# x loaded in fp32 by SyncE and cast on chip, with the constants first on GpSimd, in an attention and Fourier-mixing FFN kernel

## The chip, the cores and the metric

The kernel runs on one core of a Trainium2 chip. The metric is the device time of one execution in microseconds (us); runs are repeated and their median is taken. The engines are TensorE (PE; PEld is its weight load), VectorE (DVE), ScalarE (ACT), GpSimd (POOL) and SyncE (SP). Each has one queue of instructions that it takes in order, and a DMA stands in the queue of the engine that issues it.

## The reference

Eight batches, each with H = 8 heads of S = 512 rows of D = 64, and 32 state rows per head. First cross attention in both directions, then a mixing block over the 544 rows of 512 columns that result: the real part of a two-dimensional Fourier transform is added, the sum is normalised, and an FFN of width 2048 follows.

```python
scores = scale * np.matmul(x, state.transpose(0, 1, 3, 2))      # a  = softmax(scores)
xread = np.matmul(a, state)
scores2 = scale * np.matmul(state, x.transpose(0, 1, 3, 2))     # a2 = softmax(scores2)
sread = np.matmul(a2, x)
y = np.concatenate([xread, sread], axis=2)                      # heads side by side: (8, 544, 512)
mixed = np.real(np.fft.fft(np.fft.fft(y, axis=1), axis=2))
u = y + mixed
un = (u - mean(u)) / np.sqrt(var(u) + 1e-06)
out = u + np.maximum(un @ w_ch1, 0.0) @ w_ch2
```

## The kernel before

A batch goes through `front(b)` and then `ffn(b)`. The loop calls, for each b, `load_x(b + 2)`, `front(b + 1)` and `ffn(b)`; after batches 3 and 7 a small `front_low` and `ffn` handle the low-frequency rows of four batches together. The program is written with a scheduler that orders the instructions of each engine when the kernel is built, by the dependencies and its own idea of the times; the order on an engine is then fixed. So an instruction may stand in its queue ahead of one that the text has earlier, as the load of x for batch b + 2 does.

x is held in two buffers `xin` in bf16, [128, 4, 514]: four groups of 128 rows, with a column of ones at either end for the sums of the softmax. `load_x` (L64 to L74) fills one by five DMAs on GpSimd's queue that convert fp32 to bf16 on the way. Row 0 of x goes to partition 0 of group 2, so that group is loaded as a one-row and a 127-row piece; the others are whole 128-row pieces. The weights w1 and w2 are converted in the same way (L84, L87: four DMAs and two).

`front(b)` transposes the state and x on TensorE (`sTp` L219, `xTp` L228, with the identity matrix `ident`), copies the results to `sT` and `xT`, and computes the scores both ways (`eTp`, `esp`), the exponentials on ScalarE (`ET`, `E`), and the reads (`srp` L260, the last use of `xin`, and `xfp`, `xrp`, `xlp` L271). VectorE normalises these to XF, XR and XL and folds them into `Sm`, XE and XO (L303 to L308). GpSimd copies two columns of `Sm` and one of XL into `XN` (L306, L309). The first Fourier transform is the matmuls `gep` (L317) and `gop` (L323, and L327 with XN) against cosine and sine tables CT, ST, CL, SL; ScalarE copies them to G. The second is `yp` (L338) against T2. VectorE adds this into U (three buffers, L332), takes statistics (GpSimd finishes `rstd`, L202 and L203) and subtracts the mean; TensorE transposes (`tp`, L352) and ScalarE copies to `unT` (three buffers).

`ffn` (L387) computes 64 matmuls `ph` (L393) into `hT` (two buffers), with the ReLU on ScalarE and VectorE, and 64 matmuls `po` (L402) in four tiles. VectorE makes `ot` from `po`, `rstd` and U (L405, three buffers), and SyncE stores it, half of the tiles by way of the scratch tensor `r_dram` (L408 to L415).

At the start, GpSimd's queue has in the text `load_x(0)`, the w1 loads, `load_x(1)`, the w2 loads, the identity (L90), small constants (L110 to L115), the clears of CL and SL, the index tables by `iota` (L126 to L132), and the clears of all XF, XR, XL, XE, XO and XN buffers (L177). VectorE turns the indices into angles (`turn`, L140 to L151) in scratch of a pool `gen` of its own, and ScalarE takes the sines (L156 to L165).

Of the kernel before, what the change touches and what calls it, by code (L numbers as in the profile page):

```python
# [28 lines left out]
def kernel(  # L29
# [80 lines left out]
    epst = singles.tile([128, 1], F32, name="epst")  # L110
    nc.gpsimd.memset(epst, eps)
    mhalf = singles.tile([128, 1], F32, name="mhalf")
    nc.gpsimd.memset(mhalf, -0.5)
    halfpi = singles.tile([128, 1], F32, name="halfpi")
    nc.gpsimd.memset(halfpi, PI / 2)  # L115
# [3 lines left out]
    with tc.tile_pool(name="gen", bufs=1) as gen:  # L119
        pi_ = gen.tile([128, 5], I32, name="pi_")  # L120
        pf = gen.tile([128, 5], F32, name="pf")
        li = gen.tile([128, dm], I32, name="li")
        l1 = gen.tile([128, NM], F32, name="l1")
        l2 = gen.tile([128, dm], F32, name="l2")
        lt = gen.tile([128, NM], I32, name="lt")
        nc.gpsimd.iota(pi_[:, 0:3], pattern=[[128, 3]], base=1, channel_multiplier=1)  # L126
        nc.gpsimd.iota(pi_[:, 3:5], pattern=[[128, 2]], base=0, channel_multiplier=1)
        for hh in range(4):
            nc.gpsimd.iota(pi_[32 * hh:32 * hh + 32, 2:3], pattern=[[0, 1]], base=256, channel_multiplier=1)  # L129
        nc.gpsimd.iota(lt[:, 0:256], pattern=[[1, 256]], base=1, channel_multiplier=0)  # L130
        nc.gpsimd.iota(lt[:, 256:NM], pattern=[[1, NL]], base=256, channel_multiplier=0)
        nc.gpsimd.iota(li, pattern=[[1, dm]], base=0, channel_multiplier=0)  # L132
        nc.vector.tensor_copy(pf, pi_)  # L133
        for hh in range(4):
            nc.vector.memset(pf[32 * hh:32 * hh + 1, 2:3], 0.0)
        nc.vector.tensor_copy(l1, lt)
        nc.vector.memset(l1[:, 256:257], 0.0)
        nc.vector.tensor_copy(l2, li)

        def turn(W, N, lf, cols, name):  # L140
            n = len(cols)
            f = gen.tile([128, n, W], F32, name=f"f{name}")
            q = gen.tile([128, n, W], F32, name=f"q{name}")
            for i, c in enumerate(cols):
                nc.vector.tensor_scalar(f[:, i, :], in0=lf, scalar1=pf[:, c:c + 1], scalar2=None, op0=ALU.mult)
            nc.vector.tensor_scalar(q, in0=f, scalar1=1.0 / N, scalar2=float(1 << 23), op0=ALU.mult, op1=ALU.add)
            nc.vector.tensor_scalar(q, in0=q, scalar1=float(1 << 23), scalar2=-float(N), op0=ALU.subtract, op1=ALU.mult)
            nc.vector.tensor_add(f, f, q)
            nc.vector.tensor_scalar(q, in0=f, scalar1=-1.0, scalar2=None, op0=ALU.mult)
            nc.vector.tensor_max(q, q, f)  # L150
            return f, q  # L151

        shrink = 1.0 - 1e-6
        f, q = turn(NM, Stot, l1, [0, 1, 2], "1")
        w = 2.0 * PI / Stot * shrink
        nc.scalar.activation(CT, q[:, 0:2, :], AF.Sin, bias=halfpi, scale=-w)  # L156
        nc.scalar.activation(ST, f[:, 0:2, :], AF.Sin, bias=0.0, scale=w)
        for hh in range(4):
            pq = slice(32 * hh, 32 * hh + 32)
            nc.scalar.activation(CL[pq, hh, :], q[pq, 2, :], AF.Sin, bias=halfpi[pq], scale=-w)  # L160
            nc.scalar.activation(SL[pq, hh, :], f[pq, 2, :], AF.Sin, bias=0.0, scale=w)
        f, q = turn(dm, dm, l2, [3, 4], "2")
        w = 2.0 * PI / dm * shrink
        nc.scalar.activation(T2[:, 0:2, :], q, AF.Sin, bias=halfpi, scale=-w)
        nc.scalar.activation(T2[:, 2:4, :], f, AF.Sin, bias=0.0, scale=-w)  # L165
        alt = T2[0:1, 2, :].rearrange("p (n two) -> p two n", two=2)
        nc.vector.memset(alt[:, 0, :], 1.0)
        nc.vector.memset(alt[:, 1, :], -1.0)


    def fixed(name, shape, dt, n=2, fill=0.0):
        ts = []
        for i in range(n):
            t = singles.tile(shape, dt, name=f"{name}{i}")
            letters = "abcd"[:len(shape) - 1]
            flat = t.rearrange(f"p {' '.join(letters)} -> p ({' '.join(letters)})") if len(shape) > 2 else t
            nc.gpsimd.memset(flat, fill)  # L177
            ts.append(t)
        return ts
# [26 lines left out]
    def front(b):  # L206
# [125 lines left out]
        U = wk.tile([128, 2, 2, 514], F32, name="U", tag="U", bufs=3)  # L332
        unT = wk.tile([128, DC, 512], BF16, name="unT", tag="unT", bufs=3)
# [122 lines left out]
```

## Time and profile before

| | us |
|---|---|
| median of 3 runs | 660.19 (660.08 to 660.78) |
| profiled execution, its own time | 664.54 |
| its span, first to last instruction | 661.0 |
| TensorE busy in it | 359.5 (54%), mean granted clock 0.829 |
| VectorE, ScalarE, GpSimd busy | 205.1, 130.2, 133.2 |

The busy time of TensorE is modelled for pipelined matmuls and is no measure of how near it is to its peak. GpSimd's 133.2 us hold the time in which it issues DMAs. A wait is put down to the engine that ended it; "issue" stands for time in which an engine waited for nothing that the profile shows. A line such as L327 is a line of the kernel; where one row covers several instructions, xN gives their number.

### The profile page before, as it was taken

The numbers are of one execution on the slowest core, as the hardware profiler recorded it, in microseconds if no ns is written. First come the engines' busy times: TensorE is split into PE (matmuls) and PEld (weight loads), VectorE is DVE, ScalarE is ACT, GpSimd is POOL, SyncE is SP. The second block draws the span as 40 slices with busy tenths as digits, with TensorE's granted clock in tenths as the row PEclk, the third lists the DMA queues.
The fourth block names the chain that finished last, engine by engine and source line by source line (L and its number), as shares of the span: only waits on it lengthen the run. The fifth ranks groups of instructions, "written<-read, shape, count | busy, mean of one in ns | idle before, by whom it ended". The sixth has DMA issues, their size and how long they took to land.

```text
span 661.0 us, 5124 instructions
## 1 busy us (share of the span) xinstructions
PE 359.5 (54%) x1973; PEld 181.7 (27%) x2008; DVE 205.1 (31%) x470; ACT 130.2 (20%) x217; POOL 133.2 (20%) x170
## 2 busy tenths in 40 slices
PE   0000104138349907960990767237599949989970
PEld 0000102015124403530440326014244424434440
DVE  1000095034224604440560333413451463331220
ACT  4000033014111402410350114001123411313010
POOL 4134463222411311240241111411010001000000
PEclk9999997557859956995895788558589979999995
DMA  6592662422331362243126212440020003001210
GB/s 79 10 120 6 51 90 16 10 11 16 7 13 63 50 10 10 17 61 30 8 17 11 40 48 14 41 15 16 1 78 19 1 1 112 0 34 62 90 67 35
DMA packets 170680, 22.83 MB, mean 35 GB/s; under 512 B 158112, under 2 KB 166304, under 8 KB 170656
## 3 DMA queue, kind: packets, MB, share of 16 engines
q0 software_dynamic: 159584, 8.88, 23.9%
q1 hardware_dynamic: 11072, 13.63, 5.7%
q8 instruction: 15, 0.25, 0.2%
q14 instruction: 9, 0.07, 0.0%
HBM read 21.50 MB, written 13.11 MB: 52 GB/s over the span
## 4 chain that ended last, share of the span: by engine, by line
PE 40%; issue 35%; POOL 13%; DVE 7%; ACT 2%; POOLq 0%; DVEq 0%; ACTq 0%
PE po L402 17%; PE ph L393 13%; POOL xin L74 10%; PE yp L338 3%; PE tp L352 1%; PE gop L323 1%; PE gop L327 1%; DVE XR L295 1%; DVE st L198 1%; PE eTp L237 1%; PE srp L260 1%; PE xTp L228 1%; ACT E L254 1%; DVE U L340 1%; DVE XF L278 1%
## 5 line engine op out<-in xcount | busy, mean ns | idle before, releaser
L74 POOL DMA_DIRECT2D xin<-in_x_dram x40 | 79.4, 1993 | 247.2 <-issue 181.1
L393 PE MATMUL ph<-unT,w 128*128 128x512 bf16 x496 | 125.9, 392 | 2.2 <-ACT hT L398 0.7
L402 PE MATMUL po<-w,hT 128*128 128x512 bf16 x532 | 121.8, 382 | 3.9 <-DVE ot L405 3.0
L398 ACT ACTIVATE hT<-ph 128x512 bf16<-128x512 f32 (+1 forms) x120 | 63.2, 535 | 111.7 <-PE ph L393 90.4
L393 PEld LDWEIGHTS <-w 128*128 128x128 bf16 x640 | 60.5, 102 | 61.9 <-issue 15.2
L402 PEld LDWEIGHTS <-hT 128*128 128x128 bf16 x544 | 53.5, 98 | 67.7 <-issue 6.1
L327 PE MATMUL gop<-CT,XN 128*128 128x288 bf16 x16 | 5.3, 438 | 118.4 <-POOL XN L306 118.4
L396 DVE TENSOR_SCALAR hT<-ph 128x512 bf16<-128x512 f32 (+1 forms) x40 | 24.2, 604 | 132.6 <-PE ph L393 125.9
L219 PE MATMUL sTp<-ident,stb 128*128 128x128 bf16 x32 | 3.7, 250 | 79.9 <-POOL ident masks.py:199 79.4
L340 DVE TENSOR_TENSOR U<-yp,XF 128x512 f32<-128x512 f32 x16 | 11.1, 691 | 115.8 <-PE yp L338 115.7
L327 PEld LDWEIGHTS <-XN 128*128 128x128 bf16 x24 | 2.5, 127 | 121.8 <-POOL XN L306 120.7
L405 DVE SCALAR_TENSOR_TENSOR ot<-po,rstd,U 128x512 f32<-128x512 f32 x32 | 23.2, 746 | 38.9 <-PE po L402 38.8
L202 POOL TENSOR_TENSOR rstd<-mv,epst 128x1 f32<-128x1 f32 x34 | 6.6, 195 | 135.4 <-DVE mv L200 134.9
L354 ACT COPY unT<-tp 128x512 bf16<-128x512 bf16 x32 | 17.4, 588 | 77.7 <-PE tp L352 77.6
L328 ACT CAST G<-gop 128x576 bf16<-128x576 f32 x8 | 5.1, 638 | 127.8 <-PE gop L323 127.8
L219 PEld LDWEIGHTS <-stb 128*128 128x128 bf16 x32 | 2.8, 112 | 81.0 <-issue 73.5
L133 DVE CAST pf<-pi__121 128x5 f32<-128x5 int32 x1 | 0.2, 172 | 77.4 <-POOL pi__121 L129 77.4
L338 PE MATMUL yp<-T,G 128*128 128x512 bf16 x57 | 21.9, 485 | 2.4 <-ACT unT L354 1.1
L237 PE MATMUL eTp<-xT,sT 128*128 128x288 bf16 (+1 forms) x64 | 11.5, 310 | 20.7 <-DVE xT L229 20.4
L203 POOL TENSOR_TENSOR rstd<-rstd,mhalf 128x1 f32<-128x1 f32 x34 | 21.3, 626 | 2.7
L198 DVE BATCH_NORM_STATS2 st<-U 128x6 f32<-128x512 f32 x32 | 20.4, 681 | 0.0
L352 PE MATMUL tp<-ident,ub 128*128 128x128 bf16 x128 | 12.8, 243 | 14.0 <-DVE ub L349 13.8
(108 smaller groups left out, 376.1 us busy)
## 6 DMA issues: line engine op xcount, KB each, us to landing
r_dram<-ot SPq DMA_DIRECT2D x16, 256.0 KB
out_dram<-r_dram SPq DMA_DIRECT2D x16, 256.0 KB
out_dram<-ot SPq DMA_DIRECT2D x16, 256.0 KB
xin<-in_x_dram POOLq DMA_DIRECT2D x24, 128.0 KB, 4.3
w<-in_moe_w_ch_dram POOLq DMA_DIRECT2D x4, 512.0 KB, 8.4
w<-in_moe_w_ch_dram POOLq DMA_DIRECT2D x2, 1024.0 KB, 14.3
xin<-in_x_dram POOLq DMA_DIRECT2D x8, 127.0 KB, 23.0
stf<-in_state_dram SPq DMA_DIRECT2D x1, 512.0 KB
```

The lines of the kernel that those rows point to most:

```text
L74: nc.gpsimd.dma_start(out=t[ps, si, 1:513].rearrange("p (h d) -> p h d", d=D), in_=rows)
L198: nc.vector.bn_stats(st6, u)
L203: nc.gpsimd.tensor_tensor(rstd, rstd, mhalf, op=ALU.pow)
L237: nc.tensor.matmul(eTp[:, g, lo:hi], lhsT=sT[:, 2 * g + hp, :], rhs=xT[:, 2 * g + hp, src], start=(hp == 0), stop=(hp == 1))
L338: nc.tensor.matmul(yp[:, 0, :], lhsT=G[:, c, 128 * k:128 * k + 128], rhs=T2[:, c, :], start=(c == 0), stop=(c == 3))
L340: nc.vector.tensor_add(U[:, k, 0, 0:512], yp[:, 0, :], XF[:, k, 0:512])
L352: nc.tensor.transpose(tp[:, 0, 128 * j:128 * j + 128], ub[:, 128 * j:128 * j + 128], ident)
L393: nc.tensor.matmul(ph[:, :n], lhsT=w1[:, c, f * 128:(f + 1) * 128], rhs=unT[:, c, :], start=(c == 0), stop=(c == DC - 1))
L396: nc.vector.tensor_scalar_max(hT[:, f, :n], ph[:, :n], 0.0)
L398: nc.scalar.activation(hT[:, f, :n], ph[:, :n], AF.Relu)
L402: nc.tensor.matmul(po, lhsT=hT[:, f, i * 128:(i + 1) * 128], rhs=w2[:, f, :], start=(f == 0), stop=(f == FC - 1))
L405: nc.vector.scalar_tensor_tensor(ot, in0=po, scalar=rstd, in1=u, op0=ALU.mult, op1=ALU.add)
```

## The change

x now comes in as fp32 on SyncE's queue into a staging tile `xs` (two buffers). Group 2 is loaded as whole 128 rows, x[256:384], and row 0 of x then overwrites its partition 0, where x[256] had been put. The conversion is a copy on chip: for batch 0 two groups on VectorE and two on ScalarE, for every other batch one copy of all four groups on GpSimd. `load_x(1)` is called after the set-up. On GpSimd the identity, the iotas and the small constants come first, then the weight loads, then the clears of CL and SL; of the XF to XN buffers only the parts that nothing else writes are cleared. The scratch of `turn` lies in the two `hT` buffers, and the pools `wk`, `psQ` and `psF` are opened at the start. U and unT have two buffers instead of three.

```diff
+    wk = ctx.enter_context(tc.tile_pool(name="wk", bufs=2))
+    psQ = ctx.enter_context(tc.tile_pool(name="psQ", bufs=2, space=bass.MemoryType.PSUM))
+    psF = ctx.enter_context(tc.tile_pool(name="psF", bufs=2, space=bass.MemoryType.PSUM))
+    ident = singles.tile([128, 128], BF16, name="ident")
+    make_identity(nc, ident)
...
+    nc.gpsimd.iota(pi_[:, 0:2], pattern=[[128, 2]], base=1, channel_multiplier=1)
...
+    nc.gpsimd.iota(li, pattern=[[1, dm]], base=0, channel_multiplier=0)
+    nc.gpsimd.memset(halfpi, PI / 2)
+    nc.gpsimd.memset(epst, eps)
+    nc.gpsimd.memset(mhalf, -0.5)
...
     def load_x(b):
-        t = xin_bufs[b % 2]
+        xs = wk.tile([128, 4, dm], F32, name="xs", tag="xs")
         xb = x[b].rearrange("h s d -> s h d")
         for ps, si, rows in (
             (slice(0, 128), 0, xb[1:129]),
             (slice(0, 128), 1, xb[129:257]),
+            (slice(0, 128), 2, xb[256:384]),
+            (slice(0, 128), 3, xb[384:512]),
             (slice(0, 1), 2, xb[0:1]),
-            (slice(1, 128), 2, xb[257:384]),
-            (slice(0, 128), 3, xb[384:512]),
         ):
-            nc.gpsimd.dma_start(out=t[ps, si, 1:513].rearrange("p (h d) -> p h d", d=D), in_=rows)
+            nc.sync.dma_start(out=xs[ps, si, :].rearrange("p (h d) -> p h d", d=D), in_=rows)
+        t = xin_bufs[b % 2]
+        if b == 0:
+            for si in range(4):
+                if si % 2 == 0:
+                    nc.vector.tensor_copy(t[:, si, 1:513], xs[:, si, :])
+                else:
+                    nc.scalar.copy(t[:, si, 1:513], xs[:, si, :])
+        else:
+            nc.gpsimd.tensor_copy(t[:, :, 1:513], xs)
...
-    load_x(1)
     for q in range(2):
         nc.gpsimd.dma_start(out=w2[:, q * 8:(q + 1) * 8, :], in_=w2v[:, q * 8:(q + 1) * 8, :])
-
-    ident = singles.tile([128, 128], BF16, name="ident")
-    make_identity(nc, ident)
...
+    gen1 = wk.tile([128, 4096], F32, name="gen1", tag="hT")
+    gen2 = wk.tile([128, 4096], F32, name="gen2", tag="hT")
+    l1, l2 = gen1[:, 4096 - NM:], gen2[:, 4096 - dm:]
...
+    def turn(W, N, lf, cols, scratch):
+        n = len(cols)
+        f = scratch[:, 0:n * W].rearrange("p (n w) -> p n w", w=W)
+        q = scratch[:, n * W:2 * n * W].rearrange("p (n w) -> p n w", w=W)
...
-    XFs = fixed("XF", [128, 2, 514], BF16)
...
-    XNs = fixed("XN", [128, 3, 128], BF16)
+    for i in range(2):
+        nc.gpsimd.memset(XFs[i][:, :, 512:514], 0.0)
+        nc.gpsimd.memset(XRs[i][:, :, 0:514:513], 0.0)
+        nc.gpsimd.memset(XLs[i][:, 512:514], 0.0)
+        nc.gpsimd.memset(XEs[i][:, 2, :], 0.0)
+        nc.gpsimd.memset(XOs[i][:, 2, :], 0.0)
+        nc.gpsimd.memset(XOs[i][:, 0:2, 0:1], 0.0)
+        nc.gpsimd.memset(XNs[i].rearrange("p a b -> p (a b)"), 0.0)
...
-        U = wk.tile([128, 2, 2, 514], F32, name="U", tag="U", bufs=3)
-        unT = wk.tile([128, DC, 512], BF16, name="unT", tag="unT", bufs=3)
+        U = wk.tile([128, 2, 2, 514], F32, name="U", tag="U", bufs=2)
+        unT = wk.tile([128, DC, 512], BF16, name="unT", tag="unT", bufs=2)
...
+    load_x(1)
     ready = [front(0)]
     for b in range(B):
         if b + 1 < B:
             if b + 2 < B:
-                load_x(b + 2) if b + 2 >= 2 else None
+                load_x(b + 2)
             ready.append(front(b + 1))
         ffn(*ready[b])
```

## Rows read from the trace of the kernel before

**Rows 1.** The page's busy times: us, share of the span, instructions of each engine.

```profile
PE 359.5 (54%) x1973; PEld 181.7 (27%) x2008; DVE 205.1 (31%) x470; ACT 130.2 (20%) x217; POOL 133.2 (20%) x170
```

**Rows 2.** Waits: who waited for whom, us in total, times, longest us.

```profile
PE gop L327 <- POOL XN L306: 118.4, 6, 21.1
```

**Rows 3.** Timeline of GpSimd: start, duration (us), instruction, [idle before <- what ended it].

```profile
106.70 2.32 POOL L74 DMA_DIRECT2D xin<-in_x_dram  x3 [13.10 <-PE srp L260]
112.64 6.69 POOL L74 DMA_DIRECT2D xin<-in_x_dram  x1 [3.62 <-issue]
135.66 0.90 POOL L74 DMA_DIRECT2D xin<-in_x_dram  x1 [16.34 <-issue]
136.56 0.20 POOL L306 COPY XN<-Sm 128x2 bf16<-128x2 bf16 x1
```

**Rows 4.** DMA queues between 119 and 136 us: packets, MB, share of 16 engines.

```profile
q0 software_dynamic: 16272, 0.19, 53.7%
```

**Rows 5.** Timeline of TensorE at the gop matmuls of batches 0, 5 and 6.

```profile
136.82 0.66 PE L327 MATMUL gop<-CT,XN 128*128 128x288 bf16 x2 [18.87 <-POOL XN L306]
...
439.58 0.66 PE L327 MATMUL gop<-CT,XN 128*128 128x288 bf16 x2 [19.00 <-POOL XN L306]
...
482.02 0.69 PE L327 MATMUL gop<-CT,XN 128*128 128x288 bf16 x2
```

**Rows 6.** Timeline of the start: SyncE's queue, ScalarE, GpSimd, TensorE.

```profile
0.74 0.47 SPq L55 DMA_DIRECT2D stf<-in_state_dram  x1
...
4.83 1.28 ACT L99 ACT_TABLE_LOAD   x1 [4.83 <-DMA stf<-in_state_dram]
...
51.74 6.68 POOL L74 DMA_DIRECT2D xin<-in_x_dram  x1 [10.44 <-issue]
...
77.69 0.24 POOL masks.py:197 MEMSET ident<- 128x128 bf16 x1
...
79.41 0.59 PE L219 MATMUL sTp<-ident,stb 128*128 128x128 bf16 x4 [79.41 <-POOL ident masks.py:199]
```

**Rows 7.** Timeline of VectorE's table work, and TensorE behind it.

```profile
81.47 0.17 DVE L133 CAST pf<-pi__121 128x5 f32<-128x5 int32 x1 [77.38 <-POOL pi__121 L129]
...
90.36 1.30 DVE L146 TENSOR_SCALAR q<-f 128x1024 f32<-128x1024 f32 x1
...
92.55 0.70 DVE L147 TENSOR_SCALAR q<-q 128x1024 f32<-128x1024 f32 x1
...
98.12 0.27 DVE L168 MEMSET T<- 1x256 bf16 x1
...
101.30 2.13 PE L237 MATMUL eTp<-xT,sT 128*128 128x288 bf16 x8 [19.60 <-DVE xT L229]
```

**Rows 8.** DMA queues between 0.5 and 5 us, and between 77 and 92 us.

```profile
q1 hardware_dynamic: 2064, 0.52, 51.9%
...
q0 software_dynamic: 2986, 2.19, 108.7%
```

**Rows 9.** Groups by line and shape: busy us, mean ns | idle before, releasers.

```profile
L329 POOL COPY GL<-G 128x128 bf16<-128x128 bf16 x8 | 2.3, 290 | 22.5 <-ACT G L328 22.5
...
L116 POOL MEMSET CL<- 128x1152 bf16 x1 | 1.1, 1101 | 0.0
...
L349 DVE TENSOR_SCALAR ub<-U,mv 128x512 bf16<-128x512 f32 x32 | 14.5, 478 | 0.1
```

**Rows 10.** Windows: length, busy PE, PEld, DVE, ACT, POOL, clock, DMA share, GB/s.

```profile
190.40:193.00 2.60, 2.32 (x8) 1.33 (x10) 0.00 (x0) 0.64 (x1) 0.30 (x3) 0.50 0.79 50
...
195.00:197.00 2.00, 2.00 (x8) 0.73 (x7) 2.00 (x5) 0.60 (x1) 0.00 (x0) 0.64 0.00 0
...
461.00:484.00 23.00, 13.81 (x78) 8.36 (x78) 11.29 (x28) 4.70 (x7) 0.61 (x3) 0.52 0.03 12
```

**Rows 11.** Timeline of TensorE where batch 4 passes batch 2.

```profile
368.34 1.06 PE L338 MATMUL yp<-T,G 128*128 128x512 bf16 x2
...
375.34 10.52 PE L402 MATMUL po<-w,hT 128*128 128x512 bf16 x47 [1.44 <-DVE ot L405]
```

More of the change, by code (lines that the diff above doesn't have):

```diff
@@ L51 @@
     singles = ctx.enter_context(tc.tile_pool(name="singles", bufs=1))
+    wk = ctx.enter_context(tc.tile_pool(name="wk", bufs=2))
[3 more added lines that the diff above has]
+    make_identity(nc, ident)
+    epst = singles.tile([128, 1], F32, name="epst")
+    mhalf = singles.tile([128, 1], F32, name="mhalf")
+    halfpi = singles.tile([128, 1], F32, name="halfpi")
+    pi_ = singles.tile([128, 5], I32, name="pi_")
+    li = singles.tile([128, dm], I32, name="li")
+    lt = singles.tile([128, NM], I32, name="lt")
+    nc.gpsimd.iota(pi_[:, 0:2], pattern=[[128, 2]], base=1, channel_multiplier=1)
+    nc.gpsimd.iota(pi_[:, 3:5], pattern=[[128, 2]], base=0, channel_multiplier=1)
+    for hh in range(4):
+        nc.gpsimd.iota(pi_[32 * hh:32 * hh + 32, 2:3], pattern=[[0, 1]], base=256, channel_multiplier=1)
+    nc.gpsimd.iota(lt[:, 0:256], pattern=[[1, 256]], base=1, channel_multiplier=0)
+    nc.gpsimd.iota(lt[:, 256:NM], pattern=[[1, NL]], base=256, channel_multiplier=0)
+    nc.gpsimd.iota(li, pattern=[[1, dm]], base=0, channel_multiplier=0)
+    nc.gpsimd.memset(halfpi, PI / 2)
+    nc.gpsimd.memset(epst, eps)
+    nc.gpsimd.memset(mhalf, -0.5)
     stf = singles.tile([128, B, 2, D], F32, name="stf")
@@ L109 @@
     T2 = singles.tile([128, 4, dm], BF16, name="T2")
[L110 to L115, printed above, removed]
     nc.gpsimd.memset(CL.rearrange("p a b -> p (a b)"), 0.0)
     nc.gpsimd.memset(SL.rearrange("p a b -> p (a b)"), 0.0)
[L119 to L168, printed above, removed]
@@ L171, in fixed @@
[L171 to L179, printed above, removed]
-    XFs = fixed("XF", [128, 2, 514], BF16)
-    XRs = fixed("XR", [128, 2, 514], BF16)
-    XLs = fixed("XL", [128, 514], BF16)
@@ L184 @@
-    XEs = fixed("XE", [128, 3, 256], BF16)
-    XOs = fixed("XO", [128, 3, 256], BF16)
-    XNs = fixed("XN", [128, 3, 128], BF16)
+    pf = singles.tile([128, 5], F32, name="pf")
+    gen1 = wk.tile([128, 4096], F32, name="gen1", tag="hT")
+    gen2 = wk.tile([128, 4096], F32, name="gen2", tag="hT")
+    l1, l2 = gen1[:, 4096 - NM:], gen2[:, 4096 - dm:]
+    nc.vector.tensor_copy(pf, pi_)
+    for hh in range(4):
+        nc.vector.memset(pf[32 * hh:32 * hh + 1, 2:3], 0.0)
+    nc.vector.tensor_copy(l1, lt)
@@ new lines @@
+    nc.vector.memset(l1[:, 256:257], 0.0)
+    nc.vector.tensor_copy(l2, li)
+    def turn(W, N, lf, cols, scratch):
+        n = len(cols)
+        f = scratch[:, 0:n * W].rearrange("p (n w) -> p n w", w=W)
+        q = scratch[:, n * W:2 * n * W].rearrange("p (n w) -> p n w", w=W)
+        for i, c in enumerate(cols):
+            nc.vector.tensor_scalar(f[:, i, :], in0=lf, scalar1=pf[:, c:c + 1], scalar2=None, op0=ALU.mult)
+        nc.vector.tensor_scalar(q, in0=f, scalar1=1.0 / N, scalar2=float(1 << 23), op0=ALU.mult, op1=ALU.add)
+        nc.vector.tensor_scalar(q, in0=q, scalar1=float(1 << 23), scalar2=-float(N), op0=ALU.subtract, op1=ALU.mult)
+        nc.vector.tensor_add(f, f, q)
+        nc.vector.tensor_scalar(q, in0=f, scalar1=-1.0, scalar2=None, op0=ALU.mult)
+        nc.vector.tensor_max(q, q, f)
+        return f, q
@@ new lines @@
+    shrink = 1.0 - 1e-6
+    f, q = turn(NM, Stot, l1, [0, 1, 2], gen1)
+    w = 2.0 * PI / Stot * shrink
+    nc.scalar.activation(CT, q[:, 0:2, :], AF.Sin, bias=halfpi, scale=-w)
+    nc.scalar.activation(ST, f[:, 0:2, :], AF.Sin, bias=0.0, scale=w)
+    for hh in range(4):
+        pq = slice(32 * hh, 32 * hh + 32)
+        nc.scalar.activation(CL[pq, hh, :], q[pq, 2, :], AF.Sin, bias=halfpi[pq], scale=-w)
+        nc.scalar.activation(SL[pq, hh, :], f[pq, 2, :], AF.Sin, bias=0.0, scale=w)
+    f, q = turn(dm, dm, l2, [3, 4], gen2)
@@ new lines, with two @@
+    w = 2.0 * PI / dm * shrink
+    nc.scalar.activation(T2[:, 0:2, :], q, AF.Sin, bias=halfpi, scale=-w)
+    nc.scalar.activation(T2[:, 2:4, :], f, AF.Sin, bias=0.0, scale=-w)
+    alt = T2[0:1, 2, :].rearrange("p (n two) -> p two n", two=2)
+    nc.vector.memset(alt[:, 0, :], 1.0)
+    nc.vector.memset(alt[:, 1, :], -1.0)
+    def two(name, shape):
+        return [singles.tile(shape, BF16, name=f"{name}{i}") for i in range(2)]
+    XFs, XRs, XLs = two("XF", [128, 2, 514]), two("XR", [128, 2, 514]), two("XL", [128, 514])
@@ new lines @@
+    XEs, XOs, XNs = two("XE", [128, 3, 256]), two("XO", [128, 3, 256]), two("XN", [128, 3, 128])
+    for i in range(2):
[6 more added lines that the diff above has]
+        nc.gpsimd.memset(XNs[i].rearrange("p a b -> p (a b)"), 0.0)
@@ L187 @@
     GLs = [singles.tile([128, 4, 128], BF16, name=f"GL{i}") for i in range(2)]
-    wk = ctx.enter_context(tc.tile_pool(name="wk", bufs=2))
-    psQ = ctx.enter_context(tc.tile_pool(name="psQ", bufs=2, space=bass.MemoryType.PSUM))
-    psF = ctx.enter_context(tc.tile_pool(name="psF", bufs=2, space=bass.MemoryType.PSUM))
     def q2(name, dt=F32):
```

## The prediction

> **What bounds the kernel now.** I read four views, in this order. The page's busy times come first: TensorE carries the most work, 359.5 us, and yet only 54% of the span [rows 1], so some 300 us go to waiting and the question is what for. The list of waits answers most of it. One wait of TensorE is worth 118.4 us in six pieces: the `gop` matmuls of L327 wait for GpSimd's `XN` copies of L306 [rows 2]. The copies are 0.2 us; the GpSimd timeline of one batch shows what stands ahead of them in the queue [rows 3]. At 106.70, as soon as `srp` has let go of `xin`, the load of x for two batches later begins: three DMAs in 2.32 us, a pause of 3.62, the 127-row DMA in 6.69, a pause of 16.34, one DMA in 0.90, and only then, at 136.56, the copy that batch 0 needed. The pause is the 127-row DMA draining: between 119 and 136 us the software queue moves 16272 packets of together 0.19 MB, some 12 bytes each, and holds 53.7% of 16 engines [rows 4]. 127 x 512 / 4 = 16256, so this piece travels four elements at a time. The reader sees it from the other end on TensorE: 18.87 us idle at the first `gop`, 19.00 at the sixth, six of them; in batch 6, which has no load beside it, the same line starts at once [rows 5], and in batch 7 likewise.
>
> The other block is the start. Loads of x for batches 0 and 1 go through the same queue; the second 127-row DMA is issued at 51.74 after 10.44 us of pause, the identity matrix behind it is made at 77.69, and TensorE first runs at 79.41 [rows 6]. The first constants reach VectorE at 81.47 after 77.38 us of idling; it makes the tables until 98.39, then copies sT and xT, and TensorE's `eTp` starts at 101.30 [rows 7]. From there to the end of the span are 661.0 - 101.30 = 559.7 us, with the 118.4 in them.
>
> **The change part by part.**
> *The x loads leave GpSimd.* Per batch GpSimd loses 2.32 + 6.69 + 0.90 = 9.9 us of issue and 3.62 + 16.34 = 20.0 us of pauses [rows 3]. SyncE gets five issues instead. `stf` is the model: a 512 KB load in 256-byte runs on SyncE's queue, issued in 0.47 us at 0.74 and in use at 4.83 [rows 6], 2064 packets and 0.52 MB, no splitting [rows 8]. An x piece is half of it, so 4 pieces (1 MB) take about twice the 4.1 us of `stf`, 4 to 8 us. The one-row DMA overwrites part of piece 2 and must wait for it: at most the 4.1 us of `stf` again, by my estimate half, in which SyncE's queue, the output stores included, stands. The stores hide that: `ot` has three buffers and a tile of `po` (16 matmuls of about 0.22 us, from 47 in 10.52 [rows 11]) comes only every 3.5 us. The loads of b+2 need only a staging buffer, free when the cast of batch b is done, so I expect them on SyncE well ahead of need.
>
> *The cast takes the place on GpSimd.* 2048 elements per partition, fp32 to bf16. No row shows it. The nearest are the GL copy, 0.29 us for 128 elements, and a clear of 1152 in 1.10 us [rows 9]: 0.95 ns per element gives 2.0 us, the copy's whole duration per element (2.27 ns) gives 4.6. I take 2, because most of the small copy is fixed time (a copy of 2 elements takes 0.20 [rows 3]). It can start when `srp` ends, at 106.70 in batch 0, and the `XN` copies are wanted by TensorE at 136.82 - 18.87 = 117.95 [rows 3, 5]: 11.2 us of cover, so either end costs nothing, provided x has landed. The cast of batch 1 has the whole start as cover. Queued behind a late cast would be `XN`, with TensorE behind it, and the `rstd` pairs. So the 118.4 us go; next in line for `gop` is then the VectorE chain that makes `Sm`, `XE` and `XO`, which [rows 5] shows in time for batch 6.
>
> *The clock.* [...] I take 10.
>
> *The start.* Identity, iotas and small constants come first on GpSimd, so VectorE's table work can begin when its clears of `stb` are done, about 4 us. The chain took 98.39 - 81.47 = 16.9 us; two casts of x on VectorE add about 0.5 each (as `ub`, 0.478 [rows 9]; ScalarE makes the other two beside them), the copies of sT and xT about 1.1: `eTp` at 4 + 16.9 + 1 + 1.1 = 23. The cast of piece 2 needs the one-row DMA, at 11 to 16 us; stood VectorE's queue on it, some us more. I take 26. Lower bound 20: part of the chain ran beside GpSimd's clears, where a table operation on 128x1024 took 1.30 us and the next one, nearly clear of them, 0.70 [rows 7]. Upper bound 38: the six weight loads now stand ahead of the clears of `CL` and `SL`, for which ScalarE's sines wait; if GpSimd pauses there as it did for 10.44 us at 51.74 [rows 6], `eTp` comes 12 us later. The weights themselves stay hidden: 4.2 MB at the 2.19 MB in 15 us of [rows 8] are in by about 35 us, and `ph` starts some 30 us after `eTp`.
>
> *Fewer clears, scratch in the FFN buffers, pools opened earlier:* nothing beyond the start. The cover is the some 50 us between the tables and the first write of `hT`; without it that write would wait for the sines.
>
> *Two buffers of U and unT instead of three.* Front b+2 can write U only after the last `ot` of ffn b. In batch 4 the third buffer is in use: `yp` runs at 368.34 and 47 `po` matmuls of batch 2 only at 375.34 [rows 11]. The order will be another there; work for TensorE exists on both sides (ffn b+1 beside the U part of front b+2), so I take 0. The bounds: front 6 ran with nothing beside it, 23 us for 13.81 of work at clock 0.52, or 7.2 at full clock [rows 10], a loss of 16. Fronts 5, 6 and 7 are exposed like this, 1 to 4 nearly not. So between -48 (all three get cover) and +64 (the other four lose it).
>
> **Sum**, against the profiled execution's span: 26 + 559.7 - 118.4 - 10 = 457.3 us. The span was 661.0 and the median of the runs 660.19 beside a profiled time of 664.54, so I take off 0.8: **456.5 us**.
>
> [...] Rows 7 show that neighbours on GpSimd slow VectorE, 1.30 against 0.70 us. [...]
>
> **The rivals.**
> 1. *Cast and VectorE exclude each other.* Between 2.0 and 4.6 us, say 3, for each of six casts on a front's chain: 456.5 + 18 = 475. For it: [rows 7]. [...]
> 2. *Two buffers uncover the early fronts.* 456.5 + 64 = 520; with two of the four, 489. For it: exposed fronts exist already [rows 10]. Against: ffn b+1 is ready to run.
> 3. *The limit evens the order.* All three late fronts get cover: 409.
> 4. *x queues behind the output stores.* If SyncE's order puts the load of b+2 behind the last store of ffn b-1, the cast, and with it `XN` and `gop`, wait for landing and cast, about 9 + 2 us in each of six batches: 456.5 + 66 = 522. Against: the load has no such dependency, and the loads of before were moved ahead of later work.
> 5. *The cast holds GpSimd as long as the DMA did, and the kernel gets slower.* Place: ahead of `XN`, six batches. The cover is 11 us; the gains are 204, or 34 per batch, so it decides from a cast of 45 us, 22 ns per element. The dearest price from rows is 2.27 ns.
>
> That the change doesn't do what it says is hard to see: whole 128-row pieces have a precedent in `stf`.
>
> **How the numbers follow.** Forecast 0.61, rival 1 0.07, rival 2 0.11, rival 3 0.08, rival 4 0.09, rival 5 0.03, and 0.01 for a mixture that ends level. Low end 428: start at 20 and one and a half late fronts covered. High end 512: start at 38, no clock gain, two early fronts uncovered (32), which leaves out rival 4 and the worst of rival 2. 0.2% of 660 us is about what a measurement of this kernel tells from no change: faster 0.96, same 0.01, slower 0.03.
>
> **What would show it.** In the changed kernel `gop` should wait for `XN` under 1 us per batch (rivals 4 and 5: 10 us or more, after a cast that waits for a DMA, or a long cast); software packets should fall to those of the weights; the cast should read about 2 us; `eTp` should start between 20 and 38 us; the clock should stay at full speed through the middle batches. Wrong would be fronts 1 to 4 with TensorE idle and nothing beside them, or a wait of U for `ot`. The weakest term is the order of instructions, worked out from buffers alone.

## The result and the profile after

The changed kernel takes **468.86 us** in the median of 4 runs (467.91 to 469.21), the kernel before 660.13 beside them (659.60 to 660.78): a ratio of 0.710, 95% interval 0.709 to 0.711. The forecast was 456.5 us, with a range of 428 to 512. The profiled execution took 467.91 us, its span 466.0.

The page of the changed kernel: span, busy us of each engine (share, instructions), the granted clock in 40 slices (tenths), and the queue that GpSimd's DMAs use (packets, MB, share of 16 engines).

```profile
span 466.0 us, 5169 instructions
...
PE 348.8 (75%) x2008; PEld 175.3 (38%) x2008; DVE 204.3 (44%) x472; ACT 134.2 (29%) x221; POOL 58.7 (13%) x139
...
PEclk9999988999999999999987899999989977889985
...
q0 software_dynamic: 4192, 4.19, 5.4%
```

TensorE has the same work as in [rows 1] in 195 us less, GpSimd less than half. The 16272-packet loads of [rows 4] are gone: the 4192 packets left are the weights. The clock is full through most of the middle and falls in the last quarter; the dip in slices 21 to 23 is the front of batch 5, which has no other matmul beside it (from 250 to 260 us TensorE is busy 5.75 us at a granted clock of 0.51).

Groups by line and shape in the changed kernel: busy us, mean ns | idle before, releasers. They answer [rows 2] and [rows 9].

```profile
L107 POOL CAST xin<-xs 128x2048 bf16<-128x2048 f32 x7 | 13.2, 1893 | 73.7 <-DMA xs<-in_x_dram 41.6 <-PE srp L266 32.1
...
L333 PE MATMUL gop<-CT,XN 128*128 128x288 bf16 x16 | 4.1, 346 | 0.0
...
L312 POOL COPY XN<-Sm 128x2 bf16<-128x2 bf16 x8 | 2.0, 247 | 144.4 <-DVE Sm L309 144.4
```

`gop` waits 0.0 us for XN where it waited 118.4 [rows 2]; the XN copies now wait for VectorE's `Sm`, as the prediction had it. The cast takes 1.89 us (forecast 2.0).

The start of the changed kernel, timelines of GpSimd, ScalarE, VectorE and TensorE: start, duration, instruction, [idle before <- what ended it]. They answer [rows 6, 7].

```profile
6.27 1.80 POOL L119 DMA_DIRECT2D w<-in_moe_w_ch_dram  x2
...
23.86 0.62 ACT L105 CAST xin<-xs 128x512 bf16<-128x512 f32 x1 [11.62 <-DMA xs<-in_x_dram]
...
38.53 1.28 ACT L173 ACT_TABLE_LOAD   x1
...
43.33 1.28 ACT L260 ACT_TABLE_LOAD   x1
...
30.78 0.43 DVE L103 CAST xin<-xs 128x512 bf16<-128x512 f32 x1 [11.34 <-DMA xs<-in_x_dram]
...
31.27 1.67 PE L234 MATMUL xTp<-ident,xin 128*128 128x128 bf16 x14 [20.58 <-DVE xin L103]
...
34.98 1.01 PE L243 MATMUL eTp<-xT,sT 128*128 128x288 bf16 x4 [2.04 <-DVE xT L235]
...
45.70 1.90 PE L266 MATMUL srp<-xin,E 128*128 128x257 bf16 x8 [7.60 <-ACT E L260]
```

GpSimd has issued the last weight load at 8.07 without a pause, and yet `eTp` starts at 34.98, not 26: the casts of x(0) on ScalarE and VectorE wait 11 us for their data. The DMA queues between 6 and 24 us say why (q1 is SyncE's, q0 GpSimd's):

```profile
q0 software_dynamic: 2779, 2.78, 92.7%
q1 hardware_dynamic: 2821, 0.71, 28.8%
```

The DMA engines are full, each of the 40 slices of this window 90% busy or more. The weights' packets are 1 KB and x's 256 bytes, and the two queues get nearly the same number of packets; so x(0), 1 MB, gets a fifth of the bytes and lands at 30.8. After `eTp` there is a second loss: ScalarE's eight sines for CL and SL stand between its two exponentials, with a table load on either side, and `srp` waits 7.60 us.

From `eTp` to the end are 466.0 - 35.0 = 431.0 us, forecast 431.3. That agreement is worth less than it looks, as the experiments show. In e1 below the profiled execution ran at a lower granted clock than the others (0.748 against 0.908 to 0.932) and took longer (557.47 us), so only its start is used, and its time and stretch come from the other three (spans of 480.7 to 484.2).

### The profile page after: what moved, and what is told of

Its sections match the earlier page's. It is cut to its first block, busy times and chain, and to the rows that moved or that the text cites. A ratio compares the mean times of both kernels' runs of the same rounds, so it can differ in the third digit from the quotient of the medians.

```text
span 466.0 us, 5169 instructions
## 1 busy us (share of the span) xinstructions
PE 348.8 (75%) x2008; PEld 175.3 (38%) x2008; DVE 204.3 (44%) x472; ACT 134.2 (29%) x221; POOL 58.7 (13%) x139
## 3 DMA queue, kind: packets, MB, share of 16 engines
q0 software_dynamic: 4192, 4.19, 5.4%
## 5 line engine op out<-in xcount | busy, mean ns | idle before, releaser
L408 PE MATMUL po<-w,hT 128*128 128x512 bf16 x544 | 126.2, 381 | 5.4 <-DVE ot L411 5.4
L399 PE MATMUL ph<-unT,w 128*128 128x512 bf16 x512 | 123.5, 384 | 0.2
L234 PE MATMUL xTp<-ident,xin 128*128 128x128 bf16 x128 | 12.0, 248 | 22.5 <-DVE xin L103 20.6
L346 DVE TENSOR_TENSOR U<-yp,XF 128x512 f32<-128x512 f32 x16 | 11.1, 691 | 27.4 <-PE yp L344 27.2
L325 ACT CAST G<-gep 128x576 bf16<-128x576 f32 x8 | 5.1, 638 | 61.7 <-PE gep L323 61.7
L107 POOL CAST xin<-xs 128x2048 bf16<-128x2048 f32 x7 | 13.2, 1893 | 73.7 <-DMA xs<-in_x_dram 41.6
L358 PEld LDWEIGHTS <-ub 128*128 128x128 bf16 x128 | 8.3, 104 | 33.0 <-DVE ub L355 32.5
L312 POOL COPY XN<-Sm 128x2 bf16<-128x2 bf16 x8 | 2.0, 247 | 144.4 <-DVE Sm L309 144.4
L236 ACT COPY xT<-xTp 128x1024 bf16<-128x1024 bf16 x8 | 8.1, 1009 | 41.4 <-DVE xT L235 41.4
L269 DVE RECIPROCAL rcs<-srp 128x2 f32<-128x2 f32 x8 | 1.4, 171 | 41.7 <-PE srp L266 41.7
L234 PEld LDWEIGHTS <-xin 128*128 128x128 bf16 x128 | 9.9, 114 | 23.6 <-DVE xin L103 20.8
```

What stands on the lines that cost most here:

```text
L107: nc.gpsimd.tensor_copy(t[:, :, 1:513], xs)
L234: nc.tensor.transpose(xTp[:, g, o:o + 128], xin[:, si, 1 + 128 * pr:129 + 128 * pr], ident)
L358: nc.tensor.transpose(tp[:, 0, 128 * j:128 * j + 128], ub[:, 128 * j:128 * j + 128], ident)
L399: nc.tensor.matmul(ph[:, :n], lhsT=w1[:, c, f * 128:(f + 1) * 128], rhs=unT[:, c, :], start=(c == 0), stop=(c == DC - 1))
L408: nc.tensor.matmul(po, lhsT=hT[:, f, i * 128:(i + 1) * 128], rhs=w2[:, f, :], start=(f == 0), stop=(f == FC - 1))
```

## The experiments

The table divides each kernel at `eTp`: its start and the stretch from there to the end of the profiled span.

| kernel | median us | `eTp` at | from `eTp` to the end |
|---|---|---|---|
| before | 660 to 661 | 101.3 | 559.7 |
| the change | 468.86 | 35.0 | 431.0 |
| e1 shape only | 485.92 | 53.4 | 427 to 431 |
| e2 e1, two buffers | 454.60 | 53.5 | 399.8 |
| e3 weights after x(0) | 448.08 | 19.9 | 426.7 |
| e4 clears first | 456.60 | 28.5 | 427.5 |
| e5 converted, GpSimd | 431.89 | 21.6 | 408.2 |
| e6 fp32, GpSimd | 431.21 | 27.6 | 402.6 |
| e7 127 rows, SyncE | 483.69 | 51.5 | 430.1 |
| e8 cast twice | 473.91 | 34.6 | 437.9 |
| e9 stores on GpSimd | 434.23 | 34.1 | 398.4 |
| e10 e5, three buffers | 462.18 | 21.6 | 435.8 |
| e11 e6, cast twice | 430.50 | 27.4 | 401.3 |
| e12 e6, 127 rows | 583.12 | 49.8 | 531.8 |

### e1 and e2: the shape alone, and two buffers on top

e1 is the kernel before with one edit; x is still converted by GpSimd's DMAs. e2 also has `bufs=2` for U and unT.

```diff
-            (slice(0, 1), 2, xb[0:1]),
-            (slice(1, 128), 2, xb[257:384]),
+            (slice(0, 128), 2, xb[256:384]),
             (slice(0, 128), 3, xb[384:512]),
+            (slice(0, 1), 2, xb[0:1]),
```

> The kernel before, with one edit: group 2 of x is loaded as whole 128 rows and row 0 then over its partition 0; the loads stay on GpSimd's queue and convert on the way, no cast on chip, constants behind the loads as before. The orders on TensorE, VectorE and ScalarE are those of before. Theory 'the 127-row piece is the whole cause': the waits of gop for XN go (118.4 us), the pauses at the start too, GpSimd then needs some 13 us of issue ahead of the identity, eTp follows 22 us behind that at 36 to 48 us, and 559.7 - 118.4 - 10 = 431 us later it ends: 467 to 479 us, as fast as the whole change. Theory 'the queue is the cause' (any x load ahead of XN holds GpSimd): each batch still waits for the drain of four pieces, 5 us or more at gop, 500 to 560 us.

> As e1_shape_only, with two buffers of U and unT instead of three. Against e1: rival 2 (the limit uncovers the early fronts) +32 to +64 us; rival 3 (it evens the order) -16 to -48 us; my forecast, that it is worth nothing, within 5 us of e1. The changed kernel took about 7 us less from its first ph to its end than stalls and clock account for, which speaks for a small gain.

The piece of 127 rows is nearly the whole effect: e1 runs at 485.92 us (ratio 0.734, 0.730 to 0.737), 175 of the change's 191 us, with no cast, no fp32 staging and no move to SyncE. 48 of them are the start (101.3 to 53.4, two pauses gone), some 130 the stretch behind, where the prediction had 118.4 + 10. And the two buffers, for which it had 0, are worth another 31 us (454.60; ratio 0.688, 0.686 to 0.691). e2 is then faster than the whole change in spite of a start that is 18 us later: the change must lose about 30 us behind `eTp`.

### e3 and e4: what holds x(0) up

e3 puts two tiny copies from the loaded x(0) into w1 and w2 ahead of the weight loads, which so wait for x(0). e4 clears CL and SL ahead of the weight loads, which thereby start some 2 us later. In both the sines stand in one row.

```diff
+    nc.gpsimd.tensor_copy(w1[:, 0, 0:2048:512], xin_bufs[0][:, 0:4, 1])
+    nc.gpsimd.tensor_copy(w2[:, 0:16:8, 0], xin_bufs[0][:, 2:4, 1])
```

> The changed kernel, with two tiny GpSimd copies that write one element into each part of w1 and w2 out of xin of batch 0, so that the weight loads start only when x(0) has landed and is cast. In the changed kernel x(0) shares the DMA engines with the weights until 33 us and its last piece is cast at 30.8. The order of the sines comes out different as well, so that the table loads in the middle (7.6 us of waiting for E) go. Theory 'contention with the weights sets the start': x(0) is cast by 14 us, eTp starts at 22 to 26 instead of 35.0, total 469 - 10 - 7.6 = 451 us. Theory 'the table work sets the start': eTp stays above 30, total 461. If the weights then come too late, ph of batch 0 waits for them and the total is above 465.

> The changed kernel, with the clears of CL and SL ahead of the weight loads on GpSimd. The sines of CL and SL then stand in one row with the others on ScalarE and the two extra changes of its table (2.6 us and the eight sines between ET and E) go; x(0) still shares the DMA engines with the weights. Expected: eTp about as late as now (35 us; up to 3 us later by the sines ahead of it), srp no longer 7.6 us behind, 461 to 465 us. If the detour lay beside other work, 469.

TensorE's start in e3:

```profile
15.90 1.68 PE L234 MATMUL xTp<-ident,xin 128*128 128x128 bf16 x14 [5.35 <-DVE xin L103]
19.85 1.01 PE L243 MATMUL eTp<-xT,sT 128*128 128x288 bf16 x4 [2.27 <-DVE xT L235]
```

With the DMA engines to itself x(0) is there 15 us earlier, and `eTp` starts at 19.85; the kernel takes 448.08 us (0.678, 0.676 to 0.680). In e4 even some 2 us of lead bring 6.4. `srp` comes 5.8 and 5.4 us after `eTp` (25.62, 33.97) where the change has 10.7, so the detour of the sines costs about 5. But the stretch behind is 427 in both. What e2 has over the change there lies neither in the start nor in the sines.

### e5, e6 and e9: the way x comes in

e5 has x converted by GpSimd's queue in 128-row pieces, x(0) ahead of the constants, the clears behind them. e6 is the same kernel with x in fp32 and cast on chip, but loaded by GpSimd's queue. e9 is the change with only the output stores moved, from SyncE to GpSimd. The first pair of lines is from e6 (e5 loads into `xin` itself), the second from e9, which changes the two stores by way of `r_dram` likewise.

```diff
-            nc.sync.dma_start(out=xs[ps, si, :].rearrange("p (h d) -> p h d", d=D), in_=rows)
+            nc.gpsimd.dma_start(out=xs[ps, si, :].rearrange("p (h d) -> p h d", d=D), in_=rows)
...
-                    nc.sync.dma_start(out=d[1], in_=ot[d[0], :])
+                    nc.gpsimd.dma_start(out=d[1], in_=ot[d[0], :])
```

> The changed kernel with three edits: x is loaded by GpSimd's converting DMA straight into bf16 xin as in the kernel before, but in the 128-row pieces (no fp32 buffer, no cast); the load of batch 0 stands ahead of the constants and so ahead of the weights in GpSimd's queue; the CL and SL clears stand right behind the constants, so that the sines come in one row. Two U and unT buffers as in the change. eTp should start at 20 to 26 us (19.85 with the weights held back). Theory A, that the x path over SyncE (loads behind output stores, then a cast) is what keeps the changed kernel at 427 us from eTp to the end: without it the stretch is about 400 us as in e2, and the time 422 to 430 us. Theory B, that the order of PE's instructions, which the planner sets anew with each edit, makes the 427 against 400: the stretch stays near 427 and the time is 448 to 456 us.

> The same kernel as e5, but x is still loaded in fp32 into the two staging buffers and cast on chip; the loads are issued by GpSimd's queue and not SyncE's, so none stands behind an output store. If the output stores ahead of the x loads in SyncE's queue cost the late batches, the stretch from eTp to the end is about 400 us here too and the time 424 to 432 us. If the fp32 staging costs it (a second wait, for the cast, and a staging buffer that must come free), it stays near 427 us and the time is 448 to 456 us. If it is only the order of instructions, e5 and e6 lie within 4 us of each other near 450 us.

> The changed kernel with its output stores (three statements at the end of ffn) issued by GpSimd's queue; x stays in fp32 on SyncE's queue, with its cast, and the start is that of the changed kernel (eTp near 35 us). In the instruction order that is laid down for this kernel the xTp of batches 6 and 7 stands ahead of the FFN of the batch before, as in e6; in the changed kernel it stands behind 64 ph and some 28 to 35 po. If loads behind stores in SyncE's queue, through that order, make the 27 us between the changed kernel and e6, then eTp to the end is about 400 to 410 us and the time 437 to 448 us (the stores now stand among GpSimd's own copies, which can take some of it back: gop may wait for XN again for some us). If SyncE's loads are slow for another reason, the stretch stays near 427 us and the time at 462 to 472 us.

All three run at 431 to 434 us (ratios 0.653, 0.652 and 0.656, each within 0.003). e5 and e6 agree in the total, but not term by term: `eTp` starts 6 us earlier in e5, and then `gop` waits 8.1 us once, for an `XN` copy that stands behind loads of x on GpSimd's queue. So conversion in the DMA and cast on chip come to the same here. e9 has the late start of the change and still gains 34.6 us: **x's loads and the output stores in one queue** cost the change about 30 us (from `eTp` to the end, e9 is 32.6 us shorter and e6 28.4). The mechanism can be read in the traces. The changed kernel at batch 6, GpSimd and TensorE:

```profile
283.01 1.89 POOL L107 CAST xin<-xs 128x2048 bf16<-128x2048 f32 x1 [7.89 <-DMA xs<-in_x_dram]
...
288.81 14.31 PE L399 MATMUL ph<-unT,w 128*128 128x512 bf16 x64
304.57 7.71 PE L408 MATMUL po<-w,hT 128*128 128x512 bf16 x35 [1.44 <-DVE ot L411]
312.12 1.06 PE L234 MATMUL xTp<-ident,xin 128*128 128x128 bf16 x16
```

SyncE's queue in the changed kernel, with the last two of the five pieces of x(6) among the stores:

```profile
225.80 0.42 SPq L98 DMA_DIRECT2D xs<-in_x_dram  x1
...
260.32 12.28 SPq L414 DMA_DIRECT2D out_dram<-ot  x10
272.65 1.92 SPq L98 DMA_DIRECT2D xs<-in_x_dram  x1
```

TensorE and GpSimd in e6:

```profile
188.03 1.89 POOL L82 CAST xin<-xs 128x2048 bf16<-128x2048 f32 x1 [10.64 <-PE srp L266]
...
277.87 1.06 PE L234 MATMUL xTp<-ident,xin 128*128 128x128 bf16 x16
278.97 0.81 PE L399 MATMUL ph<-unT,w 128*128 128x512 bf16 x3
```

In e6 x(6) is cast at 188, and `xTp` of batch 6 opens a stretch in which the front alternates with the 64 `ph` and the `po` of batch 5. In the changed kernel the pieces of x(6) stand among the stores and the cast comes at 283. And `xTp` stands behind all 64 `ph` and 35 `po`. At run time nothing waits for it any more: at 312.12 the cast has been done for 27 us. So the order was laid down when the kernel was built; that the late place of the loads made it so is read from the orders, and e9, which moves only the stores and gets the early order back, bears it out. By then only some `po` are left to fill the front, and the same happens in batch 7. Windows of that front, batch 7, in both kernels: length, busy PE, PEld, DVE, ACT, POOL, clock, DMA share, GB/s; first the changed kernel, then e6.

```profile
365.40:398.50 33.10, 19.91 (x121) 10.30 (x120) 16.61 (x43) 6.40 (x9) 3.83 (x11) 0.81 0.00 1
```

```profile
322.10:366.00 43.90, 40.93 (x239) 20.19 (x241) 22.30 (x52) 14.46 (x24) 3.84 (x11) 1.00 0.10 37
```

TensorE is idle for 13 of 33 us at a clock of 0.81, against 3 of 44 at full clock. In e9 `xTp` of batches 6 and 7 stands ahead of the `ph` again, as in e6. What the loads themselves would cost if only their order on SyncE changed, with TensorE's order kept, wasn't tried; the trace shows no wait of TensorE for them after the start.

### e10: the third buffer again

```diff
-        U = wk.tile([128, 2, 2, 514], F32, name="U", tag="U", bufs=2)
-        unT = wk.tile([128, DC, 512], BF16, name="unT", tag="unT", bufs=2)
+        U = wk.tile([128, 2, 2, 514], F32, name="U", tag="U", bufs=3)
+        unT = wk.tile([128, DC, 512], BF16, name="unT", tag="unT", bufs=3)
```

> e5 (x converted by GpSimd's queue, 128-row pieces, constants and clears first) with three U and unT buffers instead of two. TensorE's order is then instruction for instruction that of e1. If the third buffer lets the fronts be laid out early, in one piece and with no FFN matmul beside them, as e1 against e2 suggests (31 us), the time is 455 to 466 us, the clock falls where those fronts stand, and PE waits longer for VectorE and ScalarE in them. If the 31 us came from something else in e1 (GpSimd's pause at the start, the clears), e10 lies within 5 us of e5, at 427 to 437 us; if a third buffer helps, as the prediction allowed (up to 48 us with late fronts covered), below 427 us.

462.18 us against 431.89: the third buffer costs 30.3 us (7%), as 31 between e1 and e2. The front of batch 6 in e10, TensorE's timeline and then its window:

```profile
259.94 1.86 PE L225 MATMUL xTp<-ident,xin 128*128 128x128 bf16 x16
262.66 2.06 PE L234 MATMUL eTp<-xT,sT 128*128 128x288 bf16 x8 [0.85 <-DVE xT L226]
...
266.81 1.06 PE L257 MATMUL srp<-xin,E 128*128 128x257 bf16 x8 [1.24 <-ACT E L251]
...
276.90 0.66 PE L314 MATMUL gep<-CT,XE 128*128 128x288 bf16 x2 [2.36 <-DVE XE L301]
```

```profile
259.40:281.50 22.10, 13.06 (x82) 8.10 (x82) 11.29 (x28) 4.72 (x7) 0.99 (x4) 0.62 0.04 14
```

No `ph` or `po` stands in it: 22 us at clock 0.62, close to the 23 us at 0.52 of the kernel before [rows 10]. The same front in e5:

```profile
279.37 1.06 PE L225 MATMUL xTp<-ident,xin 128*128 128x128 bf16 x16
280.48 0.81 PE L390 MATMUL ph<-unT,w 128*128 128x512 bf16 x3
```

As I read the orders, with a buffer free the front is laid out at once and in one piece; with two it must wait for U, and by then FFN matmuls are there to stand beside it. Fronts 6 and 7 get their cover so. Front 5 gets none with two buffers either: in e6 TensorE is busy 5.30 us from 239 to 249, at clock 0.53, as in the changed kernel.

### e8 and e11: the price of the cast

Both do the cast of batches 1 to 7 twice, e8 in the changed kernel, e11 in e6.

```diff
             nc.gpsimd.tensor_copy(t[:, :, 1:513], xs)
+            nc.gpsimd.tensor_copy(t[:, :, 1:513], xs)
```

> The changed kernel with GpSimd's cast of x done twice for each of batches 1 to 7 (7 more casts at 1.89 us, 13.2 us of GpSimd time). If the cast lies beside other work, as the prediction took it, with 11.2 us of cover: 468 to 470 us. If every cast stands on the path: 482 us. If only the late batches 6 and 7, where the load lands late, wait for it: 471 to 473 us. If GpSimd's cast holds VectorE up by more than its own length, above 482 us.

> e6 (x in fp32 on GpSimd's queue, cast on chip) with the cast of batches 1 to 7 done twice. Here the orders of PE, VectorE and ScalarE are instruction for instruction those of e6, while in e8 the second cast also moved 38 rows of PE's order. If a cast lies beside other work, the time is that of e6 within 1 us (430 to 433 us), and the 5 us of e8 came by the order. If each cast costs its 1.89 us on the path, 444 us; if only those that wait for PE's srp just ahead of the next xTp, 433 to 440 us. If GpSimd's cast and VectorE keep each other off the memory, VectorE's operations beside a cast take 1.9 us longer each and the time is above 440 us.

e8 costs 5.05 us more, e11 nothing (430.50 against 431.21). The difference is again the order: e11 has the order of e6 on TensorE, VectorE and ScalarE instruction for instruction, while in e8 the `xTp` of batches 6 and 7 moved behind 7 and 8 more `po`, probably because the second cast made them later in the plan. Groups of e11, the two casts:

```profile
L82 POOL CAST xin<-xs 128x2048 bf16<-128x2048 f32 x7 | 13.5, 1934 | 47.3 <-PE srp L267 46.9 <-PE xfp L278 0.4
...
L83 POOL CAST xin<-xs 128x2048 bf16<-128x2048 f32 x7 | 13.3, 1899 | 0.3
```

13.3 us more of GpSimd, and VectorE's busy time is 203.8 us against 203.9 in e6. So the cast lies wholly beside other work and slows VectorE by nothing that can be seen. But that is a matter of place. Of the some 56 VectorE instructions that run beside a cast in e11, all but two read PSUM. In e9 four of the seven casts come later, beside the small VectorE sum of two SBUF inputs that completes XE. GpSimd, VectorE and TensorE of e9, with the cast of x(4) in the front of batch 2:

```profile
128.53 1.98 POOL L107 CAST xin<-xs 128x2048 bf16<-128x2048 f32 x1
...
128.79 1.87 DVE L313 TENSOR_TENSOR XE<-XL 32x256 bf16<-32x256 bf16 x1
...
130.71 0.30 PE L323 MATMUL gep<-CL,XE 128*128 128x288 bf16 x1 [1.60 <-DVE XE L313]
```

The sum takes 0.28 us in e6 and 1.86 to 1.97 in these four, until the cast is done, and TensorE waits 5.8 us for it in all. At the start of the changed kernel a VectorE conversion of 128x288 takes 4.32 us beside GpSimd's clears, and 0.31 in e3, where the clears are over by then. The 128x1024 operation that took 1.30 us beside clears [rows 7] takes 0.69 in the changed kernel, at 15.53, where they are over. So GpSimd did hold VectorE in these places; the cast was free in e11, where all but two of the instructions beside it read PSUM, and cost 5.8 us in e9, where it stood beside the sum for XE.

### e7 and e12: 127 rows on either queue, without conversion

```diff
-            (slice(0, 128), 2, xb[256:384]),
-            (slice(0, 128), 3, xb[384:512]),
             (slice(0, 1), 2, xb[0:1]),
+            (slice(1, 128), 2, xb[257:384]),
+            (slice(0, 128), 3, xb[384:512]),
```

> The changed kernel, with x's third piece again cut as in the kernel before, row 0 and then 127 rows at partition 1, in fp32 on SyncE's queue. If the cost of before lay in 127 rows that a converting GpSimd load cuts into packets of some 12 bytes, the fp32 load keeps its packets of 256 bytes, at worst all 1016 of them on one DMA engine (about 16 us at the 2 us that 128 packets on each engine took for the state), beside other work: 468 to 485 us, and GpSimd's XN copies wait no longer than in the changed kernel. If a piece of 127 rows is slow on any queue, the loads take as long as before, fronts wait for x and the time goes to 560 to 600 us.

> e6 with x's third piece cut again in row 0 and 127 rows at partition 1, in fp32 on GpSimd's queue. If it is the conversion of 127 rows that made packets of some 12 bytes before, the packets stay as large as those of e6 and the 254 KB go through one DMA engine at about 18 GB/s, as e7 showed on SyncE's queue: 14 us for each batch, hidden but for the first, so 444 to 450 us. If GpSimd's queue cuts any piece of 127 rows in that way, some 16000 to 32000 packets for each batch, 16 us or more with all engines filled, GpSimd pauses again and XN comes late: 480 to 560 us.

On SyncE's queue (e7, the change otherwise) the piece costs 14.8 us, all of it at the start. GB/s in 40 slices of the window 30.5 to 46 us, and then VectorE's cast that waits for the piece:

```profile
GB/s 13 13 13 11 13 13 11 13 17 18 18 18 18 18 18 18 18 18 18 18 18 18 18 18 18 18 18 18 18 18 18 18 18 18 94 165 279 206 107 236
```

```profile
45.59 0.43 DVE L103 CAST xin<-xs 128x512 bf16<-128x512 f32 x1 [29.97 <-DMA xs<-in_x_dram]
```

The piece runs alone at 18 GB/s, where 128-row pieces behind it reach 279; a sixteenth of 279 is 17.4, so by my estimate from these two rates one DMA engine of the 16 carries the piece.

SyncE's queue is stopped by the piece too. These are the DMAs right behind it, for batches 0 and 2, where the median DMA of x takes 0.85 us to issue:

```profile
5.53 37.64 SPq L98 DMA_DIRECT2D xs<-in_x_dram  x1
...
63.73 14.01 SPq L98 DMA_DIRECT2D xs<-in_x_dram  x1
```

The first stands while the weights load as well. The later stops cost nothing, because no copy that TensorE waits for stands behind them in this queue.

On GpSimd's queue (e12, e6 otherwise) it costs 152 us. GpSimd's timeline, and the DMA queue between 162 and 177 us:

```profile
154.92 6.69 POOL L73 DMA_DIRECT2D xs<-in_x_dram  x1 [0.73 <-issue]
178.24 2.67 POOL L73 DMA_DIRECT2D xs<-in_x_dram  x3 [16.63 <-issue]
180.91 0.21 POOL L312 COPY XN<-Sm 128x2 bf16<-128x2 bf16 x1
```

```profile
q0 software_dynamic: 1029, 0.32, 50.1%
```

These are the 6.69 us of [rows 3], the pause is within 0.3 us of the 16.34 there, and `gop` waits 112.5 us for XN, near the 118.4 of [rows 2]. The packets are others: 1029 with 0.32 MB, not 16272 with 0.19 [rows 4]. Each of these counts mixes two kinds. By size, the trace of e12 has 63 packets of 4096 bytes in this window, the size of the 128-row pieces in e6, and 942 of 64 bytes; the kernel before has 1016 of 128 bytes, the size of its 128-row pieces too, and 15256 of 4 bytes. So the data of the piece goes in packets as large as those of the other pieces, and small ones come on top; what those are for, the traces don't say.

The pause is the piece draining, as I had it: the last packets start at 135.0 and 177.5, the next DMA at 135.66 and 178.24. But its reason is neither the conversion nor the number of packets. The 127-row piece stopped the queue that it stood in, GpSimd's for 16.34 us in the kernel before and 16.63 in e12, SyncE's for 14.01 in e7, and on GpSimd's queue the `XN` copies stand behind it. Whether the 127 rows or the start at partition 1 make it wasn't tried apart.

## Why the prediction was right

**The bound and the main term: right.** The XN wait is gone to the last tenth, next in line is the `Sm` chain, the cast takes 1.89 us under its cover, and the clock stays full in the middle but for front 5. 118.4 + 10 was forecast for the stretch; e1, which takes only the pauses away, gained about 130. The 10 us for the clock no run shows by themselves: [rows 10] have 0.50 and 0.64 behind one wait, and what e1 showed is 10 to 14 us beyond the 118.4, at a mean granted clock of 0.91 to 0.93 in its three runs against 0.83 to 0.87 before. One reading on the way was wrong: some 12 bytes is the mean of packets of 128 and of 4 bytes, so the piece does not travel "four elements at a time", and that 127 x 512 / 4 comes near the count shows nothing of it.

**The start: 9 us too early.** `eTp` came at 34.98, inside the bounds of 20 to 38, but the step failed. I gave x(0) "4 to 8 us" and the one-row piece behind it up to 16, from `stf`, beside which the other queue moved only 0.12 MB between 0.5 and 5 us, and called the weights hidden because they are not needed early. They are hidden, but not free: they take the DMA engines from x(0). My reason for the upper bound, a pause of GpSimd, did not occur. The step on VectorE ("stood VectorE's queue on it, some us more") did, at 11.34 us. The order of the sines, about 5 us, I had left out; the bound named the clears, not the table loads.

**Two buffers: wrong, and hidden by a second error.** I took 0 between -48 and +64. Where x comes by GpSimd's queue, e10 and e2 show -30: rival 3, to which I gave 0.08, is the mechanism, for two of its three fronts. **x behind the output stores** is rival 4, to which I gave 0.09, and it is there too, with another price and place than I wrote: about 30 us in the last two batches, not 11 us in each of six, and not as a wait for landing but through TensorE's order. Both meet in the same fronts, 6 and 7: two buffers give them their cover, and the loads behind the stores take it away again. So the two cancel to within some us, and the stretch came out at 431.0 against 431.3; this is put together from the other kernels, as the change with three buffers wasn't run. The forecast of the total was good for a reason I did not have. My argument against rival 4, that the load depends on no store, was true and beside the point: in SyncE's queue ten stores stood from 260.32 to 272.60 us ahead of the last piece of x(6), and the plan follows the queue.

Rival 1 fell for the change: `XE`, `XO` and `Sm` never run beside a cast there, and in e11 a second cast costs nothing. Its mechanism is real, though: in e9, where the cast stands beside `XE`, it costs TensorE up to 1.6 us for each of four casts (rival 1 took 3). Rival 2 fell with the sign of the buffers. Rival 5 fell with the cast's 1.89 us. The bounds of the total are each 1.5 us from what their terms add up to (426.5 and 510.5), which changes nothing. "The weakest term is the order of instructions" was the right warning.

The best versions, e5 and e6, keep the 128-row piece, the constants ahead of the weights and two buffers, and take x off SyncE's queue: 431 us, 8% below the change. The fewer clears, the scratch in the `hT` buffers and the earlier pools were not run apart; e5 has them and e2 hasn't, and their stretches differ by 8.4 us, of which the one wait of 8.1 for `XN` is nearly all.

## What to carry to other kernels

Look at the number of rows of a slow load before its queue or its type, and at what stands behind it in its queue: one row more, overwritten afterwards, was worth 175 us here. Keep loads that open the next stage in a queue without stores (some 30 us here), and ask of every early bulk load whose DMA time it takes, even if nobody waits for it (15 us of `eTp` in e3). Where a scheduler lays down the order, a change of a few us in a load, a copy or a buffer can move whole stages in the order, so compare the orders before you price the edit.

## What the runs showed of the hardware

- The 127-row load stopped the next DMA of the queue that it stood in: on GpSimd's queue for 16.34 us converted to bf16 (the kernel before) and 16.63 in fp32 (e12), on SyncE's for 14.01 us (e7, where it ran at 18 GB/s).
- In the changed kernel two DMA queues with 1 KB and 256-byte packets got 2779 and 2821 packets between 6 and 24 us, 2.78 and 0.71 MB: the shares went by packets there, not bytes.
- GpSimd's fp32 to bf16 copy took 0.92 ns per element and partition (1.893 us for 2048), near its clear (0.95, [rows 9]). Beside it a VectorE sum of two SBUF inputs took 1.87 us instead of 0.28 (e9). In e11, where all but two of some 56 VectorE instructions beside it read PSUM, VectorE was busy 203.8 us, against 203.9 in e6.
- A VectorE conversion of 128x288 took 4.32 us beside GpSimd's clears (the changed kernel) and 0.31 without them (e3).
